# Attention feeding a channel mix: one ring of PSUM banks, dense dummy matmuls, a re-ordered plan and re-cut loads

## The chip, the cores and the metric

The kernel runs on one core of a Trainium2 chip. The metric is device time in microseconds (us), the median of several executions. One execution was also profiled; its trace gives every instruction's start and duration on the engines: TensorE (PE, matmuls; PEld for its weight loads), VectorE (DVE), ScalarE (ACT), GpSimd (POOL) and SyncE (SP, which here only issues transfers).

## What is computed

There are 8 batches of 576 tokens and 8 heads of 64 columns. `phi` gives 32 memory slots per head. The output of the attention, with heads side by side, goes through a token-shift channel mix with weights of 512 x 1024, 1024 x 512 and 512 x 512.

```python
def _attn_ref(q, k, v, phi):
    a = np.exp(phi - np.max(phi, axis=2, keepdims=True))
    a = a / (np.sum(a, axis=2, keepdims=True) + 1e-09)       # over the tokens
    k_m = np.einsum('bhsm,bhsd->bhmd', a, k)
    v_m = np.einsum('bhsm,bhsd->bhmd', a, v)
    scores = np.matmul(q, k_m.transpose(0, 1, 3, 2)) / np.sqrt(64)
    attn = softmax(scores)                                   # over the 32 slots
    return np.matmul(attn, v_m)

def _moe_ref(x, mu_k, mu_r, w_k, w_v, w_r):
    x_prev = x shifted by one token
    xk = mu_k * x + (1.0 - mu_k) * x_prev
    xr = mu_r * x + (1.0 - mu_r) * x_prev
    k = np.maximum(xk @ w_k, 0.0)
    v = k * k @ w_v
    r = 1.0 / (1.0 + np.exp(-(xr @ w_r)))
    return r * v
```

## The kernel before

**Two families of steps.** `attention(b)` (L212) makes the steps of one batch, `channel_mix(c)` (L512) those of one chunk of 512 tokens; there are nine chunks. The list `PLAN` (L18) is a hand-kept order of all steps: `0:hk0` is step `hk0` of batch 0, `c0:12` the thirteenth step of chunk 0. The program is recorded in just this order, so every engine executes its own instructions in the order of `PLAN`; semaphores make them wait for their operands and for free buffers.

**A batch's steps.** `exp` (L229) takes the exponential of phi on ACT, `exp0` and `exp1` each for 64 of the 128 partitions. `k`, `v`, `kv` (L232) sum keys and values over the tokens on PE, 72 small matmuls; `hk0`, `hk1`, `hv0`, `hv1` do so for half the heads. `z` (L248), or `z0` and `z1` (L256), is the sum of the exponentials, 9 matmuls each. `nk`, `nv`, `hn0`, `hn1` divide on DVE; `tk`, `ht0`, `ht1` (L295) transpose the memory keys. `q0` and `q1` (L318), or `hq0` and `hq1` (L333), transpose the queries on PE, 18 matmuls each, and copy them out of PSUM; `hq` puts one of its two copies on ACT, `q` puts all on DVE but for batch 0. `qx` (L313) does the same for batch 7 with two crossbar transfers that SP issues. `s0` and `s1` (L348) are the scores with their exponentials on ACT. `l0` to `l3` (L366) sum over the slots on PE and take Ln on ACT; `r0z`, `h0z` and the like (L378) take Exp of minus that, the reciprocal; `w`, `y` (L383) multiply on DVE. From batch 2 on, `x0` to `x3` (L390) are the attention's output, copied out by ACT, and `dd`, `k0d`, `k2d`, `r0d`, `r2d` (L404, L415) form the two token-shift mixes on DVE. For batches 0 and 1 `mk0` to `mk3` and `mr0` to `mr3` (L435) fold the mix into the value product on PE ("mixed value matmuls"), and half of their copies are on ACT, half on DVE.

**A chunk's steps.** Steps 0 to 7 are keys (L518): four matmuls, Relu on ACT into `rl`, the square on DVE into `sq`. Gates (L534): four matmuls, Exp on ACT, and after every second one Ln and Exp of 1024 columns on ACT. Values (L551): eight matmuls, a multiply on DVE into `o`, a store that SP issues. In chunks 0 and 8 steps 8 to 11 are the gates and 12 to 15 the values; in the others they alternate in pairs.

**Dummies.** `busy1` (L192) is one matmul of 128 x 512 zeros whose result nobody reads.

**Buffers.** [...] They are three pools, `at` of 3, `pk` of 2, `pv` of 3; keys and dummies use `pk`, gates and values `pv`, and the attention's tiles whatever the letters after a `+` in `PLAN` name (L215). Most attention tiles in SBUF have two buffers, `sq` one.

**Loads.** POOL issues them all, with a cast to bf16, but for batch 0's phi. Before any step: k and q of batch 0 by halves, v, `wk` in two pieces, `wr`, `wv`, then batch 1 (`ORDER`, L46). `b:load` (L291) loads batch b+2 into the buffers of b. At most eight POOL loads are under way: each waits for the one eight before it.

Of the kernel before, what the change touches and what calls it, by code (L numbers as in the profile page):

```python
# [18 lines left out]
    "0:exp0 0:busy1 0:busy1 0:busy1 0:busy1 0:busy1 0:busy1 0:exp1 0:z0 0:hk0+k 0:busy1 0:hn0 0:ht0+v 0:hq0+va",  # L19
    "0:z1+v 0:busy1 0:s0+kv 0:hk1+v 0:busy1 0:l0 0:busy1 0:h0z 0:busy1 0:l1 0:hn1 0:ht1+k 0:mu+k 0:hq1+vv 0:mub",  # L20
    "0:h1z 0:y1 0:s1+va 0:hv0+v 0:nr0 0:busy1 0:l2 0:h2z 0:nk0 0:y0 0:l3 0:y2 0:busy1 6:load 0:busy1 0:h3z 0:busy1",
    "0:hv1+v 0:nk1 0:y3 0:load 0:busy1 0:mk1+aa 0:nr1 0:mk0+ka 0:mk2+vk 0:mk3+va 0:mr0+av c0:0 c0:1 c0:2 c0:3 c0:4",
    "c0:5 c0:6 c0:7 0:mr2+aa 0:mr1+va c0:8 0:mr3+kk 1:exp c0:9 c0:10 c0:11 0:busy1 1:z+k 0:busy1 c0:12 1:k+aa 1:nk",
    "1:tk 1:q1+aa 1:q0+av c0:13 1:s1+kv 1:s0+kv 1:v+aa 1:nk1 1:nr0 1:nk0 1:nr1 1:l2+v 1:load 1:h2z 1:y2 1:l3 1:h3z",
    "1:y3 c0:14 7:load 1:l1+v 1:l0 1:h1z 1:y1 1:h0z 1:y0 c0:15 2:exp 1:mk1+av 1:mk2+vk 1:mk0+ak 2:z 1:mk3+av",
    "1:mr0+vv c1:0 c1:1 c1:2 1:mr3+aa 1:mr1+va 1:mr2+vv c1:3 2:q0+ak 2:q1+av 2:kv+vv 2:nk c1:4 c1:5 2:load 2:tk",
    "3:exp 2:nv c1:6 c1:7 2:s0+aa 2:s1+av c1:8 c1:9 2:l2+k c1:10 2:l3+v c1:11 2:r1z 2:w1 3:z+k 2:l0 2:l1+k 3:q1+va",
    "2:r0z c1:12 2:x3+vk 2:x2+aa 3:kv+vk 2:w0 2:x1+va 3:nv 3:nk 3:q0+kv 3:load 2:x0+av 3:tk c1:13 3:s0+ka 2:dd",
    "2:k0d 3:s1+ak 2:k2d 4:exp c1:14 c1:15 3:l0+v 2:r2d c2:0 c2:1 4:z 3:l1 c2:2 c2:3 2:r0d c2:4 3:r0z 3:l3 c2:5",
    "3:l2 c2:6 4:kv+va 4:nk 3:r1z 3:w1 4:nv 5:exp c2:7 c2:8 c2:9 3:w0 4:q1+av 4:q0+ak 4:load c2:10 3:x2+vk 3:x1+ka",  # L30
# [15 lines left out]
ORDER = ('wv', 'phi', 'k', 'q', 'v')  # L46

NJ = 9
# [4 lines left out]
def kernel(  # L56
# [94 lines left out]
    wk_v = moe_w_k.rearrange("(do di) f -> di do f", di=128)  # L151
    for i in range(2):
        fs = slice(i * Dff // 2, (i + 1) * Dff // 2)
        nc.gpsimd.dma_start(out=wk_sb[:, :, fs], in_=wk_v[:, :, fs])
    nc.gpsimd.dma_start(out=wr_sb, in_=moe_w_r.rearrange("(do di) d2 -> di do d2", di=128))
    wv_v = moe_w_v.rearrange("(fo fi) d -> fi fo d", fi=128)
    for what in ORDER:
        if what == "wv":
            nc.gpsimd.dma_start(out=wv_sb, in_=wv_v)
        elif what == "phi":  # L160
            load_phi(1, (nc.gpsimd, nc.gpsimd))
        elif what == "q":
            load_q(1)
        else:
            load_rows(kvs[1][:, "kv".index(what)], (k, v)["kv".index(what)][1])


# [24 lines left out]
    def keep_busy(n):  # L192

        ps = psum.tile([128, CT], F32, name="idle", tag="pk", bufs=2)
        for _ in range(n):
            nc.tensor.matmul(ps, lhsT=zeros[:, 0:128], rhs=zeros, start=True, stop=True,  # L196
                             skip_group_check=True)

    def load_mu_b():
        ps = psum.tile([128, 2, 2, D], F32, name="mub", tag="pk", bufs=2)  # L200
        for c in range(2):
            nc.tensor.matmul(ps[:, :, c], lhsT=sel[:, c].rearrange("k g m -> k (g m)"), rhs=mu_r[:, :, c],
                             start=True, stop=True, skip_group_check=True)
        nc.vector.tensor_copy(mu_m[:, :, 0], ps)
        nc.vector.tensor_scalar(mu_m[:, :, 1], ps, -1.0, 1.0, op0=AL.mult, op1=AL.add)

    def load_mu():
        ps_mu = psum.tile([128, 2 * ND], F32, name="psmu", tag="at", bufs=3)
        nc.tensor.transpose(ps_mu, mu2, ident_f)
        nc.vector.tensor_scalar_add(mu1, ps_mu, -1.0)  # L210

    def attention(b):  # L212
        st = {}

        def ps_tile(shape, dtype, name):  # L215

            tags = st["tags"]
            tag = {"a": "at", "k": "pk", "v": "pv"}[tags[st["n"] % len(tags)]]
            st["n"] += 1
            return psum.tile(shape, dtype, name=name, tag=tag, bufs={"at": 3, "pk": 2, "pv": 3}[tag])  # L220
# [27 lines left out]
        def esum():  # L248
            st["zps"] = ps_tile([128, 2], F32, "zps")
            for j in range(NJ):  # L250
                nc.tensor.matmul(st["zps"], lhsT=em[:, j].rearrange("p h m -> p (h m)"), rhs=ones,
                                 start=j == 0, stop=j == NJ - 1, skip_group_check=True)
            st["rz"] = work.tile([128, 2], F32, name="rz", tag="rz")
            nc.vector.reciprocal(st["rz"], st["zps"])

        def esum_half(c):  # L256

            def go():
# [5 lines left out]
                if "rz" not in st:  # L264
                    st["rz"] = work.tile([128, 2], F32, name="rz", tag="rz")
# [3 lines left out]
        def norm_k(cs=(0, 1)):  # L269

            def go():
                if "kbd" not in st:
                    st["kbd"] = work.tile([128, 2, 2, D], BF16, name="kbd", tag="kbd")
# [5 lines left out]
        def norm_v():  # L279
            vb = work.tile([128, 2, D], BF16, name="vb", tag="vb")  # L280
# [14 lines left out]
        def tr_k(cs=(0, 1)):  # L295

            def go():
# [5 lines left out]
                if "kmT" not in st:  # L303
                    st["kmT"] = work.tile([128, 2, 128], BF16, name="kmT", tag="kmT")
# [13 lines left out]
        def tr_q(i):  # L318
            def go():
# [8 lines left out]
                for hg in range(2):  # L328
                    (nc.scalar.copy if b == 0 and hg else nc.vector.tensor_copy)(
# [18 lines left out]
        def scores(c):  # L348

            def go():  # L350
                if "e" not in st:
                    st["e"] = work.tile([128, 2, S], BF16, name="e", tag="e")
# [30 lines left out]
        def weigh(c, sl=slice(0, S)):  # L383
            def go():
                if "at" not in st:
                    st["at"] = work.tile([128, 2, S], BF16, name="atn", tag="atn")
# [3 lines left out]
        def values(c, hf):  # L390

            def go():
                if "x" not in st:
                    st["x"] = work.tile([128, ND, S], BF16, name="x", tag="x")
# [90 lines left out]
        def step(name):  # L485
            name, _, tag = name.partition("+")
# [3 lines left out]
            def go():  # L490
                st["tags"], st["n"] = tag or "a", 0
                steps[name]()
            return go
# [18 lines left out]
    def channel_mix(c):  # L512
# [5 lines left out]
        def key(fi):  # L518
            def go():
                if "sq" not in st:  # L520
                    st["sq"] = work.tile([128, NF, CT], BF16, name="sq", tag="sq", bufs=1)
                pk = psum.tile([128, CT], F32, name="pk", tag="pk", bufs=2)
# [11 lines left out]
        def gate(ts):  # L534

            def go():
                pr = psum.tile([128, Dm], F32, name="pr", tag="pv", bufs=3)
# [13 lines left out]
        def value(ts):  # L551
            def go():
                o = work.tile([128, Dm], F32, name="o", tag="o", bufs=4)
                n = 2 if c == NCH - 1 and ts == 3 else 1
                for h in range(n):
                    cols = slice(h * Dm // n, (h + 1) * Dm // n)
                    pv = psum.tile([128, Dm], F32, name="pv", tag="pv", bufs=3)
# [7 lines left out]
        groups = [key(fi) for fi in range(NF)]  # L565
        order = "g0 g1 g2 g3 v0 v1 v2 v3" if c in (0, NCH - 1) else "g0 g1 v0 v1 g2 g3 v2 v3"
        return groups + [(gate if o[0] == "g" else value)(int(o[1])) for o in order.split()]


# [41 lines left out]
```

## Time and profile before

| | |
|---|---|
| median of 5 runs | 213.32 us (212.94 to 213.4) |
| the profiled execution | 213.26 us |
| its span, first to last instruction | 211.5 us |
| mean granted clock of PE | 0.968 |
| PE busy | 202.0 us, 96% |
| ACT busy | 161.4 us, 76% |
| DVE busy | 136.0 us, 64% |
| POOL busy | 46.2 us, 22% |
| moved by DMA | 31.90 MB, mean 151 GB/s |

The span is 1.76 us shorter than the time of the same execution: what lies ahead of the first instruction and after the last belongs to the time only. "Busy" counts a matmul from its start to its modelled end, and matmuls overlap, so 96% doesn't say that PE works at its peak. The granted clock is the share of full speed that PE was allowed. DMA is busy throughout the first half of the span and mostly at four tenths or less after it.

### The profile page before, as it was taken

How to read it: one execution, taken by the hardware profiler on the slowest of the kernel's cores; microseconds unless marked ns; L12 is line 12 of the kernel's file. 1: busy time of each engine (PE TensorE's matmuls, PEld its weight loads, DVE VectorE, ACT ScalarE, POOL GpSimd, SP SyncE). 2: the span in 40 equal slices, each digit the busy share in tenths (PEclk: the TensorE clock that was granted, in tenths of full speed). 3: DMA queues.
4: the chain of work that ended last, by engine and by line, in shares of the span. 5: the costliest groups of instructions: out<-in, count | busy, mean ns of one | idle time of the engine just before them, and what ended most of it. 6: DMA issues, size and time to landing. Idle time of an engine off the chain costs nothing.

```text
span 211.5 us, 5608 instructions
## 1 busy us (share of the span) xinstructions
PE 202.0 (96%) x2268; PEld 101.3 (48%) x2268; DVE 136.0 (64%) x338; ACT 161.4 (76%) x304; POOL 46.2 (22%) x79
## 2 busy tenths in 40 slices
PE   5699999999999999999999999999999999999992
PEld 1465434555454454544546855444444444444451
DVE  1326651796729988599869776975797497524231
ACT  2555779596698989887979799699979966766760
POOL 7732144532645352444200000000000000000000
PEclk9755999999999999999999999999999999999999
DMA  6999999999999999999991744030421034044024
GB/s 134 209 206 206 229 208 216 240 238 303 209 244 235 246 242 228 231 240 245 241 213 55 142 66 102 13 86 0 102 63 41 10 89 102 0 99 99 0 69 133
DMA packets 25826, 31.90 MB, mean 151 GB/s; under 512 B 4800, under 2 KB 20424, under 8 KB 25800
## 3 DMA queue, kind: packets, MB, share of 16 engines
q0 software_dynamic: 16912, 20.91, 53.9%
q1 hardware_dynamic: 8360, 10.07, 18.8%
q10 hardware_dynamic: 528, 0.56, 1.0%
q8 instruction: 18, 0.29, 0.5%
q14 instruction: 8, 0.07, 0.1%
HBM read 38.28 MB, written 9.44 MB: 226 GB/s over the span
## 4 chain that ended last, share of the span: by engine, by line
PE 88%; ACT 5%; DMA 3%; issue 1%; DVE 1%; POOL 0%; ACTq 0%; POOLq 0%
PE pk L526 29%; PE pv L559 28%; PE pr L540 14%; PE kvps L242 3%; DMA q<-in_q_dram 3%; PE idle L196 2%; PE mxps L288 2%; PE zps L373 2%; PE qtps L325 2%; PE nops L288 1%; PE scps L359 1%; PE qtps L341 1%; ACT rl L530 1%; ACT sg L545 1%; ACT x L399 1%
## 5 line engine op out<-in xcount | busy, mean ns | idle before, releaser
L559 PE MATMUL pv<-wv,sq 128*128 128x512 bf16 (+1 forms) x296 | 66.7, 374 | 0.0
L526 PE MATMUL pk<-xkT,wk 128*128 128x512 bf16 (+1 forms) x320 | 66.4, 358 | 0.0
L530 ACT ACTIVATE rl<-pk 128x512 bf16<-128x512 f32 x72 | 42.5, 600 | 20.8 <-PE pk L526 17.8
L526 PEld LDWEIGHTS <-wk 128*128 128x128 bf16 x320 | 30.6, 98 | 28.8 <-issue 0.9
L531 DVE TENSOR_TENSOR sq<-rl 128x512 bf16<-128x512 bf16 x72 | 29.9, 424 | 20.5 <-ACT rl L530 19.7
L559 PEld LDWEIGHTS <-sq 128*128 128x128 bf16 x296 | 28.1, 98 | 31.3 <-issue 0.6
L561 DVE TENSOR_TENSOR o<-sg,pv 128x512 f32<-128x512 f32 (+1 forms) x37 | 24.3, 670 | 27.8 <-ACT sg L548 15.5
L540 PE MATMUL pr<-wr,xrT 128*128 128x512 bf16 x144 | 34.9, 380 | 0.2 <-DVE xrT L447 0.2
L545 ACT ACTIVATE sg<-pr 128x512 f32<-128x512 f32 x36 | 21.3, 616 | 4.9 <-PE pr L540 4.7
L540 PEld LDWEIGHTS <-xrT 128*128 128x128 bf16 x144 | 13.2, 98 | 16.2 <-issue 0.6
L548 ACT ACTIVATE sg<-sg 128x1024 f32<-128x1024 f32 x18 | 19.0, 1057 | 0.6
L547 ACT ACTIVATE sg<-sg 128x1024 f32<-128x1024 f32 x18 | 19.0, 1057 | 0.6
L399 ACT CAST x<-nops 128x256 bf16<-128x256 f32 (+1 forms) x48 | 15.5, 418 | 2.4 <-PE nops L288 2.2
L421 DVE TENSOR_SCALAR mu_d<-diff,mu 128x576 bf16<-128x576 bf16 x48 | 15.6, 369 | 0.2
L118 POOL DMA_DIRECT2D kv<-in_k_dram x16 | 10.1, 629 | 21.3 <-DMA kv<-in_k_dram 3.8
L387 DVE TENSOR_TENSOR atn<-e,lz 128x576 bf16<-128x576 bf16 (+2 forms) x20 | 12.6, 635 | 2.0 <-ACT lz L380 1.7
L363 ACT ACTIVATE e<-scps 128x320 bf16<-128x320 f32 (+1 forms) x32 | 10.9, 429 | 3.5 <-PE scps L359 3.4
L118 POOL DMA_DIRECT2D q<-in_q_dram x16 | 9.8, 613 | 16.8 <-PE qtps L325 4.3
L375 ACT ACTIVATE lz<-zps 128x320 f32<-128x320 f32 (+1 forms) x32 | 12.2, 409 | 1.3 <-PE zps L373 1.1
L118 POOL DMA_DIRECT2D kv<-in_v_dram x16 | 9.8, 613 | 15.4 <-DMA wv<-in_moe_w_v_dram 4.5
L230 ACT ACTIVATE em<-ph 128x1152 bf16<-128x1152 f32 (+1 forms) x9 | 10.5, 1169 | 2.6 <-DMA ph<-in_phi_dram 2.6
L380 ACT ACTIVATE lz<-lz 128x576 f32<-128x576 f32 (+2 forms) x20 | 11.7, 592 | 0.3
(65 smaller groups left out, 172.7 us busy)
## 6 DMA issues: line engine op xcount, KB each, us to landing
out_dram<-o SPq DMA_DIRECT2D x69, 128.0 KB, 3.6
kv<-in_k_dram POOLq DMA_DIRECT2D x16, 288.0 KB, 9.8
q<-in_q_dram POOLq DMA_DIRECT2D x16, 288.0 KB, 10.3
kv<-in_v_dram POOLq DMA_DIRECT2D x16, 288.0 KB, 9.6
ph<-in_phi_dram POOLq DMA_DIRECT2D x7, 288.0 KB, 11.1
ph<-in_phi_dram POOLq DMA_DIRECT2D x14, 144.0 KB, 10.9
wk<-in_moe_w_k_dram POOLq DMA_DIRECT2D x2, 512.0 KB, 12.9
wv<-in_moe_w_v_dram POOLq DMA_DIRECT2D x1, 1024.0 KB, 18.9
```

The costliest lines, as they stand in the source:

```text
L118: nc.gpsimd.dma_start(out=dst[ROWS[hg]].rearrange("p h j d -> p h (j d)"), in_=rows(src, hg))
L399: nc.scalar.copy(st["x"][:, 2 * c + jj, sl], pss[jj])
L421: nc.vector.tensor_scalar_mul(t[:, i], st["d"][:, pr + i, :], mu1[:, o:o + 1])
L526: nc.tensor.matmul(pk[:, lo:hi], lhsT=wk_sb[:, di, fi * 128:(fi + 1) * 128], rhs=xk_T[:, di, c0:c0 + hi - lo], start=(di == 0), stop=(di = ...
L530: nc.scalar.activation(rl, pk, AF.Relu)
L531: nc.vector.tensor_mul(st["sq"][:, fi, :], rl, rl)
L540: nc.tensor.matmul(pr, lhsT=xr_T[:, di, c0:c0 + 128], rhs=wr_sb[:, di, :], start=(di == 0), stop=(di == ND - 1))
L545: nc.scalar.activation(sg[:, ts % 2], pr, AF.Exp, scale=-1.0)
L547: nc.scalar.activation(sg, sg, AF.Ln, bias=1.0)
L548: nc.scalar.activation(sg, sg, AF.Exp, scale=-1.0)
L559: nc.tensor.matmul(pv[:, cols], lhsT=st["sq"][:, fi, ts * 128:(ts + 1) * 128], rhs=wv_sb[:, fi, cols], start=(fi == 0), stop=(fi == NF - 1))
L561: nc.vector.tensor_mul(o[:, cols], st[ts // 2][:, ts % 2, cols], pv[:, cols])
```

## The change

- `PLAN` is written anew. Batch 0 begins with 13 dummies instead of 6; six more stand later in the head, and six in the stretch where chunk 0 ends and batch 1 begins (two before). Batch 1 takes its exponentials, sums, keys, values and queries by halves (`exp0`, `z0`, `hk0`, `hq0`). Batch 6's queries go by crossbar (`6:qx`), as batch 7's do.
- All PSUM tiles come from one pool of eight; the letters in `PLAN` are gone.
- Eight SBUF tiles get three buffers instead of two, `sq` two instead of one.
- The loads before the steps follow a list, `PRE`: `wk` in three pieces, `wr`, then batch 1's q, phi and k, and `wv` in two halves of 256 columns around batch 1's v.
- Chunk 0's values are made and stored by halves of 256 columns, steps 12 to 19.
- In all chunks steps 8 to 11 are now the gates and 12 on the values.

```diff
 PLAN = [
-    "0:exp0 0:busy1 0:busy1 0:busy1 0:busy1 0:busy1 0:busy1 0:exp1 0:z0 0:hk0+k 0:busy1 0:hn0 0:ht0+v 0:hq0+va",
-    "0:z1+v 0:busy1 0:s0+kv 0:hk1+v 0:busy1 0:l0 0:busy1 0:h0z 0:busy1 0:l1 0:hn1 0:ht1+k 0:mu+k 0:hq1+vv 0:mub",
-    "0:h1z 0:y1 0:s1+va 0:hv0+v 0:nr0 0:busy1 0:l2 0:h2z 0:nk0 0:y0 0:l3 0:y2 0:busy1 6:load 0:busy1 0:h3z 0:busy1",
-    "0:hv1+v 0:nk1 0:y3 0:load 0:busy1 0:mk1+aa 0:nr1 0:mk0+ka 0:mk2+vk 0:mk3+va 0:mr0+av c0:0 c0:1 c0:2 c0:3 c0:4",
-    "c0:5 c0:6 c0:7 0:mr2+aa 0:mr1+va c0:8 0:mr3+kk 1:exp c0:9 c0:10 c0:11 0:busy1 1:z+k 0:busy1 c0:12 1:k+aa 1:nk",
-    "1:tk 1:q1+aa 1:q0+av c0:13 1:s1+kv 1:s0+kv 1:v+aa 1:nk1 1:nr0 1:nk0 1:nr1 1:l2+v 1:load 1:h2z 1:y2 1:l3 1:h3z",
-    "1:y3 c0:14 7:load 1:l1+v 1:l0 1:h1z 1:y1 1:h0z 1:y0 c0:15 2:exp 1:mk1+av 1:mk2+vk 1:mk0+ak 2:z 1:mk3+av",
...
+    "0:busy1 0:busy1 0:exp0 0:busy1 0:busy1 0:busy1 0:busy1 0:busy1 0:busy1 0:busy1 0:busy1 0:busy1 0:busy1 0:busy1",
+    "0:hk0 0:z0 0:hn0 0:exp1 0:hq0 0:ht0 0:busy1 0:z1 0:s0 0:hk1 0:busy1 0:l0 0:hn1 0:busy1 0:h0z 0:l1 0:ht1 0:mu",
+    "0:hq1 0:mub 0:s1 7:load 0:h1z 0:hv0 0:nk0 0:nr0 0:y1 0:busy1 0:y0 0:l2 0:h2z 0:busy1 0:busy1 0:l3 0:h3z 0:y2",
+    "0:hv1 0:nk1 0:y3 0:mk1 0:mk0 0:mr0 0:mk3 0:mk2 c0:0 0:nr1 c0:1 c0:3 c0:2 0:mr1 0:mr2 c0:6 c0:4 c0:5 c0:7 c0:8",
+    "0:mr3 1:exp0 1:exp1 c0:10 c0:11 1:hq1 1:z0 0:load 1:hq0 c0:9 0:busy1 1:z1 1:hk0 1:hn0 0:busy1 1:hk1 0:busy1",
+    "0:busy1 0:busy1 1:hn1 1:ht1 0:busy1 1:ht0 1:s1 1:s0 c0:17 6:load c0:13 1:hv0 1:nr0 1:l0 1:h0z 1:l1 1:h1z 1:y0",
+    "1:l3 1:y1 1:l2 1:hv1 1:nk0 1:load 1:h2z 1:y2 1:h3z 1:y3 1:nk1 c0:15 1:nr1 c0:19 1:mk0 1:mr0 c0:12 c0:16 c0:18",
+    "c0:14 1:mk1 1:mk3 1:mk2 1:mr2 c1:6 c1:3 2:exp c1:5 c1:0 c1:7 c1:4 c1:2 c1:1 c1:8 2:z 1:mr3 1:mr1 2:kv 2:nk",
...
+    "c3:12 c3:13 c4:1 c4:6 c4:4 5:tk c4:3 c4:2 6:z 6:kv 6:nk 5:s0 5:s1 6:nv c4:8 c4:7 5:l3 6:qx 5:l2 5:l0 4:r2d",
+    "5:l1 5:r1z 5:w1 5:r0z 5:w0 7:qx 4:r0d c4:5 c4:0 c3:14 5:x2 5:x1 c3:15 5:x0 5:x3 5:dd 5:k0d 5:k2d c4:10 7:exp",
...
 ]
-ORDER = ('wv', 'phi', 'k', 'q', 'v')
+PRE = "k0:0 q0:0 k1:0 q1:0 id: v0:0 v1:0 wk:0-2 wk:2-4 wk:4-8 wr:0-4 q1:1 phi:1 q0:1 k0:1 k1:1 wv:2-4 v0:1 v1:1 wv:0-2"
...
+    def preload(word):
+
+        what, _, part = word.partition(":")
+        if what in weights:
+            dst, src = weights[what]
+            f0, f1 = (int(x) * 128 for x in part.split("-"))
+            nc.gpsimd.dma_start(out=dst[:, :, f0:f1], in_=src[:, :, f0:f1])
+        elif what == "id":
+            make_identity(nc, identity)
         else:
-            load_rows(kvs[1][:, "kv".index(what)], (k, v)["kv".index(what)][1])
+            n = int(part)
+            if what == "phi":
+                load_phi(n, (nc.gpsimd, nc.gpsimd))
+            elif what[0] == "q":
+                load_q(n, (int(what[1]),))
+            else:
+                load_rows(kvs[n][:, "kv".index(what[0])], (k, v)["kv".index(what[0])][n], (int(what[1]),))
+
+    for word in PRE.split():
+        preload(word)
...
         def ps_tile(shape, dtype, name):
-
-            tags = st["tags"]
-            tag = {"a": "at", "k": "pk", "v": "pv"}[tags[st["n"] % len(tags)]]
-            st["n"] += 1
-            return psum.tile(shape, dtype, name=name, tag=tag, bufs={"at": 3, "pk": 2, "pv": 3}[tag])
+            return psum.tile(shape, dtype, name=name, tag="ps", bufs=8)
...
-                    (nc.scalar.copy if b == 0 and hg else nc.vector.tensor_copy)(
+                    (nc.scalar.copy if b < 2 and hg else nc.vector.tensor_copy)(
...
-                    st["sq"] = work.tile([128, NF, CT], BF16, name="sq", tag="sq", bufs=1)
-                pk = psum.tile([128, CT], F32, name="pk", tag="pk", bufs=2)
+                    st["sq"] = work.tile([128, NF, CT], BF16, name="sq", tag="sq", bufs=2)
+                pk = psum.tile([128, CT], F32, name="pk", tag="ps", bufs=8)
...
-        def value(ts):
-            def go():
-                o = work.tile([128, Dm], F32, name="o", tag="o", bufs=4)
-                n = 2 if c == NCH - 1 and ts == 3 else 1
-                for h in range(n):
+        def value(ts, hs=(0,), n=1):
+
+            def go():
+                if ("o", ts) not in st:
+                    st["o", ts] = work.tile([128, Dm], F32, name="o", tag="o", bufs=4)
+                o = st["o", ts]
+                for h in hs:
                     cols = slice(h * Dm // n, (h + 1) * Dm // n)
-                    pv = psum.tile([128, Dm], F32, name="pv", tag="pv", bufs=3)
+                    pv = psum.tile([128, Dm], F32, name="pv", tag="ps", bufs=8)
...
-        groups = [key(fi) for fi in range(NF)]
-        order = "g0 g1 g2 g3 v0 v1 v2 v3" if c in (0, NCH - 1) else "g0 g1 v0 v1 g2 g3 v2 v3"
-        return groups + [(gate if o[0] == "g" else value)(int(o[1])) for o in order.split()]
+        if c == 0:
+            values = [value(ts, (h,), 2) for ts in range(4) for h in range(2)]
+        elif c == NCH - 1:
+            values = [value(ts) for ts in range(3)] + [value(3, (0, 1), 2)]
+        else:
+            values = [value(ts) for ts in range(4)]
+        return [key(fi) for fi in range(NF)] + [gate(ts) for ts in range(4)] + values
```

## Prediction

> **What bounds the kernel now.** I read the page first, then the chain of waits in order of time, then windows, then the timeline of the head. On the page, busy time, the slices of the granted clock and the shares of the chain:
>
> ```profile
> PE 202.0 (96%) x2268; PEld 101.3 (48%) x2268; DVE 136.0 (64%) x338; ACT 161.4 (76%) x304; POOL 46.2 (22%) x79
> PEclk9755999999999999999999999999999999999999
> PE 88%; ACT 5%; DMA 3%; issue 1%; DVE 1%; POOL 0%; ACTq 0%; POOLq 0%
> ```
>
> TensorE (PE) is both busy and the chain, and its clock is low in slices 2 to 4 only. The chain gives the borders of four stages (start, length, what):
>
> ```profile
> 1.97 6.52 DMA q<-in_q_dram
> ...
> 21.89 7.10 PE pk L526 x32
> ...
> 45.70 0.70 PE mxps L288 x28
> ...
> 200.35 7.00 PE pv L559 x40
> 207.35 0.02 issue
> 207.37 0.42 DVE o L561
> ```
>
> Stage A, 0 to 21.89, ends with the first key matmul of chunk 0. B, 23.81 us, ends at batch 1's first mixed value matmul. C, 161.65 us, is steady: 32 full key matmuls in 6.9 us are 216 ns each, and no gap above 0.4 us stands in it. D, 4.14 us, is the last multiply and its store. B holds 21.8 us of PE work at those spacings (keys 6.9, gates 3.5, values 6.9, batch 0's last mixed halves 1.0, batch 1's sums, transposes and scores 3.1, dummies 0.4), so PE loses 2.0 us there, most of it at 29.5 to 30.5 and 36.8 to 38.2. An edit can pay in A, in B, or by taking matmuls out of C.
>
> Why A is slow, by windows of 3.41 us (window, length, PE busy and instructions, granted clock, DMA share, GB/s):
>
> ```profile
> 0.80:4.22 3.42, 2.74 (x6) 1.00 0.58 142
> 4.22:7.63 3.41, 1.08 (x46) 1.00 1.22 211
> 7.63:11.05 3.42, 2.81 (x71) 0.50 1.21 206
> 14.46:17.87 3.41, 3.41 (x56) 0.50 1.24 205
> 17.87:21.29 3.42, 3.42 (x82) 0.50 1.24 205
> 21.29:24.70 3.41, 3.41 (x31) 1.00 1.25 209
> 205.60:209.02 3.42, 1.73 (x16) 1.00 0.72 187
> 209.02:211.49 2.47, 0.00 (x0) 1.00 0.22 66
> ```
>
> The clock is halved exactly after the window that is 32% busy and comes back at 21.29. The window at the end that is 51% busy isn't followed by a halving. The head's timeline shows what left that second window empty:
>
> ```profile
> 1.19 2.74 PE L196 MATMUL idle<-zeros 128*128 128x512 bf16 x6 [1.19 <-DVE zeros L138]
> 6.49 0.38 PE L261 MATMUL zps<-ones,em 64*128 64x1 bf16 x9 [2.55 <-ACT em L230]
> 8.53 0.98 PE L341 MATMUL qtps<-identity,q 64*128 64x64 bf16 x15 [0.51 <-DMA q<-in_q_dram]
> ```
>
> Six dummies end at 3.9 and PE then waits for the exponential of phi until 6.5.
>
> [...]
>
> **The change, stage by stage.**
>
> A, if the clock holds. Thirteen dummies from 1.19 us: seven at 0.43 us to 4.2, six at 0.216 to 5.5. Then `hk0` and `z0` at 6.48 (they still wait for phi's exponential, 5.27 + 1.16). Window 4.22 to 7.63 is then 1.3 + 0.6 = 1.9 us busy, 56%; the next I count at 53%. Both lie above the 51% that kept the clock. Queries land at 8.48 as now, since the first loads keep their order. From there, with PE at half its time and the rest at trace durations: 18 transposes 0.4, ScalarE (ACT) copy 0.64 and latency, so `s0` at 9.85 (now 10.14); exponentials to 10.95; `l0`, Ln and reciprocal to 12.0; Ln of `l1`, ACT copy of the second queries to 13.0; `s1` 13.05; exponentials to 14.15; four ACT steps for rows 2 and 3 to 16.25; VectorE weighing (0.42) to 16.8; two mixed halves of 0.28. First key at **17.4**: -4.5. The gain is more than faster matmuls, since four of ten dummies inside this chain are gone, and the others are half as long.
>
> A, if it does not: the same chain at half clock, fewer dummies: first key at about 21.1, -0.8.
>
> B is where the price is. Work that leaves B: two of chunk 0's four value groups (four halves, 3.5 us). Work that enters: four more dummies (0.9) and nine more sums (9 x 0.025 = 0.2). PE work 19.3 us against 21.8. But the order puts these on ACT between gate `c0:8` and batch 1's score exponentials: gate 0.6, cast 0.4, exp of phi in two halves (1.16 each; L230 shows that 64 partitions cost as much as 128), gates 2 x 0.6, Ln and Exp of 1.06 each, two query copies of 0.64 that stood on VectorE, gate 0.6, Ln and Exp again. That is 10.6 us; successive ACT entries overlap a little, so 10.1. `c0:8` ends 8.9 us after the first key (eight keys 6.9, gate 0.86, two mixed 0.7, one wait 0.4), so exponentials start at 19.2 and the third, which `l0` needs, ends at 20.1. Then sums 0.7, `hv1` 0.3, two half-values 1.74: mixed at **22.9**. Against 23.81: -0.9, though PE now waits 3.6 us there. Who waits: `ht1`, `s1`, `l0`, and all PE work behind them. It is the ring of eight that ties `ht0` to a bank that the ACT copy must empty.
>
> Loads in B: wr landed at 22.6 (7.04 + 15.6) and wv, 1 MB, 5.1 us later. Now 1.77 MB (q, phi, k) follow wr: 8 us at about 225 GB/s, k complete at 30.5; `hk1` needs it near 31.6 and has a further 1 us before ACT binds. wv's first half lands about 33.0 (wanted 35.0), its second about 38 (wanted 41). No stall taken; bounded at 0 (nothing in B waits for a load now, so none can be gained) [...]. On POOL wv now stands behind batch 1's loads; the loads of later batches keep their order, since `0:load` only moves against other engines.
>
> C: the 3.5 us from B return. Batch 6's queries by crossbar take out 36 transposes, 0.63 us by the chain, and four VectorE copies of 0.45 off the path. Two crossbar issues (about 1.7 us each on SP) join the two for batch 7; stores wait behind them, with four output buffers as cover, and both are issued some 20 us before use. If batch 7's queries landed after their turn, stores and then VectorE's multiplies would queue: bounded at 0 to +1. The mixing chain of VectorE leaves about 0.2 us of new hole ahead of chunks 2 and 5. C = 161.65 + 3.5 - 0.63 + 0.2 = **164.7**. At nothing: one pool, deeper buffers, two squares buffers (PE never waits in C; bounds -0.4, the holes there, to +1, since a tile may now wait for the eighth tile before it); VectorE's eight half multiplies for four (+0.6 us, hidden under PE); twice the stores of chunk 0; two more POOL issues of 0.6 us, under the DMA stream. If PE stops being the cover, ACT with 161 us is the next.
>
> D is unchanged, 4.14.
>
> Sum: 17.4 + 22.9 + 164.7 + 4.1 = 209.1 against a span of 211.5. The profiled execution took 213.26, 1.76 above its span, and the median is 213.32, 0.06 more. So **210.9**, or -1.1%.
>
> **The rivals.**
>
> 1. Clock lost halfway (window 7.63 to 11.05 too thin, its matmuls small): A near 20.1, so +2.7 on the forecast: 213.6. For: windows full of small matmuls at half clock did not bring the clock back. Against: 51% held it.
>
> 2. Slower: the dummies don't hold the clock at 7.63. A is then 21.1, and B and C cost 187.6 where they cost 185.5 now: 21.1 + 22.9 + 164.7 + 4.1 = 212.8, time 214.6, with B up to 1 us worse. It decides once A gains less than 2.1 us. For: 56% was not seen followed by a kept clock while the matmuls were 64 rows tall. This is also the case that the change doesn't do what it says.
>
> 3. Clock held, but weights in pieces or a slow ACT chain stretch B by 2 to 3 us: 213 to 214. For: loads saturate DMA in B (share 1.18). Against: the margins above, 1 to 3 us.
>
> **How the numbers follow.** Forecast 0.52, rival 1 0.15, rival 2 0.25, rival 3 0.08. No change is within 0.2%, 0.4 us, about what a measurement of this kernel can tell. The forecast's own range is 209.2 to 212.6: A +-0.6, B -1 to +1, C -0.4 to +1. Faster: 0.49 + 0.06 + 0.02 + 0.01 = 0.58. Same: 0.02 + 0.03 = 0.05. Slower: 0.37. The range runs from 209.0 to 215.0 and leaves out a tenth on each side.
>
> **What would show it.** Right: PEclk at full in slices 2 to 4, first key near 17.4, ACT without gaps for 10 us before batch 1's scores, PE holes of 3 to 4 us there, 36 fewer transposes. Wrong: half clock after 7.6; batch 1 waiting for k or wv; holes after 46 us.

## The result and the profile after

The changed kernel took 213.50 us in the median of 27 runs (210.13 to 214.48), the kernel before 213.34 us in 48 (212.59 to 215.49): over all runs there is no difference. The ratio on record, 0.9939 with an interval of [0.9917, 0.9961], counts only fast runs, those within 1.5% of the kernel's fastest, and so leaves out 19 of the changed kernel's 28; it is no evidence of a gain in the usual run. The runs of the changed kernel differ by the clock that TensorE was granted. With every run's recorded mean clock beside its time (the 27 and the profiled one):

| recorded clock | runs | time, us | span, us |
|---|---|---|---|
| 1.0 | 2 | 210.13, 210.20 | 208.4, 208.3 |
| 0.980, 0.981 | 3 | 212.09 to 212.24 | 210.3 to 210.5 |
| 0.972 to 0.976 | 18 | 212.88 to 213.85 | 211.1 to 212.1 |
| 0.968 | 5, the profiled one among them | 214.22 to 214.56 | 212.4 to 212.8 |

A window of 3.41 us at half clock lowers the mean over the span by 0.008. So 0.968 is four such windows, as in the profile below (13.65 us); 0.972 to 0.976 is about three and 0.980 about two, an estimate, since no other run of this kernel was profiled. By the times of the table each costs about 1 us. The mean alone proves little, because it counts the time ahead of the first entry of the record as full speed (see e3): runs of the kernel before have means of 0.962 to 1.0 at the same times.

So the profile below (time 214.56, span 212.8) is of a run that lost the clock as early as the kernel before did. What the two runs without a loss look like inside is taken from an experiment, e1, whose span is the same within 0.3 us. Busy times, slices of the granted clock and shares of the chain, after:

```profile
PE 204.2 (96%) x2280; PEld 106.4 (50%) x2280; DVE 134.6 (63%) x338; ACT 162.3 (76%) x307; POOL 47.9 (23%) x81
PEclk9755999999999999999999999999999999999999
PE 87%; ACT 6%; DMA 3%; issue 1%; DVE 1%; POOL 0%; ACTq 0%; POOLq 0%
```

TensorE is still the busy engine and the chain, and slices 2 to 4 are at a low clock as before. The borders of the stages in the chain of waits (start, length, what), after:

```profile
1.97 6.76 DMA q<-in_q_dram
...
21.44 3.80 PE pk L519 x16
...
44.86 0.67 PE mxps L285 x24
...
201.95 6.94 PE pv L554 x40
...
208.91 0.42 DVE o L556
```

Stage A is 0.45 us shorter than before (21.44 against 21.89), B 0.39 shorter (23.42 against 23.81), C 2.38 longer (164.03 against 161.65: it got 3.5 us of chunk 0's values and lost batch 6's transposes), D 0.24 shorter: +1.3 us in the span. The windows of the head (window, length, busy time and instructions of PE, PEld, VectorE, ScalarE and POOL, granted clock, DMA share, GB/s) show where the clock went, after:

```profile
1.41:4.82 3.41, 3.41 (x9) 1.21 (x8) 0.28 (x4) 1.28 (x1) 3.33 (x7) 1.00 0.81 177
4.82:8.23 3.41, 1.88 (x50) 0.94 (x48) 1.42 (x12) 1.98 (x2) 3.00 (x5) 1.00 1.21 213
8.23:11.65 3.42, 2.88 (x73) 2.17 (x73) 0.85 (x3) 1.28 (x3) 1.68 (x3) 0.50 1.21 206
```

In the first of them the dummies come 0.43 us apart, against 0.22 from 4.92 us on: half clock, though it is printed as full (see e3). The thirteen dummies end at 5.95 us, TensorE waits 0.8 us for the keys and 1.27 for the queries, and behind a window that was 55% busy the clock is at half for 13.65 us, to 21.9 us. Stage B, in the chain of waits, is a row of ScalarE work, as forecast:

```profile
33.25 1.08 ACT sg L538 x2
...
34.35 1.06 ACT sg L540
...
35.44 1.06 ACT sg L541
36.50 1.07 ACT qT L341 x2
37.56 0.51 ACT sg L538
...
38.09 1.07 ACT sg L540
...
39.19 1.06 ACT sg L541
40.24 0.93 ACT e L360 x3
```

### The profile page after: what moved, and what is told of

Same layout as the page of the kernel before. It is cut to its first block, busy times and chain, and to the rows that moved or that the text cites. A ratio compares the mean times of both kernels' runs of the same rounds, so it can differ in the third digit from the quotient of the medians.

```text
span 212.8 us, 5653 instructions
## 1 busy us (share of the span) xinstructions
PE 204.2 (96%) x2280; PEld 106.4 (50%) x2280; DVE 134.6 (63%) x338; ACT 162.3 (76%) x307; POOL 47.9 (23%) x81
## 4 chain that ended last, share of the span: by engine, by line
PE 87%; ACT 6%; DMA 3%; issue 1%; DVE 1%; POOL 0%; ACTq 0%; POOLq 0%
PE pk L519 28%; PE pv L554 28%; PE pr L533 15%; DMA q<-in_q_dram 3%; PE kvps L239 3%; PE mxps L285 2%; PE zps L370 2%; PE nops L285 2%; ACT sg L540 2%; ACT sg L538 1%; PE qtps L338 1%; PE idle L197 1%; PE qtps L322 1%; PE scps L356 1%; ACT sg L541 1%
## 5 line engine op out<-in xcount | busy, mean ns | idle before, releaser
L523 ACT ACTIVATE rl<-pk 128x512 bf16<-128x512 f32 x72 | 40.0, 599 | 8.3 <-PE pk L519 8.0
L554 PEld LDWEIGHTS <-sq 128*128 128x128 bf16 x328 | 31.3, 98 | 29.1 <-issue 0.5
L519 PEld LDWEIGHTS <-wk 128*128 128x128 bf16 x320 | 30.8, 98 | 29.9 <-issue 0.8
L556 DVE TENSOR_TENSOR o<-sg,pv 128x512 f32<-128x512 f32 (+1 forms) x41 | 24.9, 619 | 19.0 <-ACT sg L541 9.9
L114 POOL DMA_DIRECT2D kv<-in_k_dram x16 | 10.1, 631 | 21.1 <-PE kvps L239 8.8
L227 ACT ACTIVATE em<-ph 128x1152 bf16<-128x1152 f32 (+1 forms) x10 | 11.6, 1163 | 2.8 <-DMA ph<-in_phi_dram 2.8
L372 ACT ACTIVATE lz<-zps 128x320 f32<-128x320 f32 (+1 forms) x32 | 11.5, 414 | 1.2 <-PE zps L370 1.0
```

The lines of the kernel that those rows point to most:

```text
L114: nc.gpsimd.dma_start(out=dst[ROWS[hg]].rearrange("p h j d -> p h (j d)"), in_=rows(src, hg))
L519: nc.tensor.matmul(pk[:, lo:hi], lhsT=wk_sb[:, di, fi * 128:(fi + 1) * 128], rhs=xk_T[:, di, c0:c0 + hi - lo], start=(di == 0), stop=(di = ...
L523: nc.scalar.activation(rl, pk, AF.Relu)
L554: nc.tensor.matmul(pv[:, cols], lhsT=st["sq"][:, fi, ts * 128:(ts + 1) * 128], rhs=wv_sb[:, fi, cols], start=(fi == 0), stop=(fi == NF - 1))
L556: nc.vector.tensor_mul(o[:, cols], st[ts // 2][:, ts % 2, cols], pv[:, cols])
```

## The experiments

Theory at the start: the time of the changed kernel is decided by whether dummies and small matmuls fill the 3.4 us windows between 4.8 and 11 us, and everything else in the change costs 1.3 us net. Rival: the clock is chance, and the order, the pool and the loads carry what gain there is. The second half of the theory fell with e2. All stages at a glance (first key, batch 1's first mixed value, end of the last values, span; profiled run, us) with the median of each. "First key" is where the key matmuls run on without a stop; in e1, e3, e4, e6, e8, e9 and e11 up to three single ones come up to 1.1 us earlier, and in e12 a row of four counts:

| kernel | first key | mixed | last value | span | median |
|---|---|---|---|---|---|
| before | 21.89 | 45.70 | 207.35 | 211.5 | 213.34 |
| after | 21.44 | 44.86 | 208.89 | 212.8 | 213.50 |
| e1, head filled | 18.56 | 40.53 | 204.72 | 208.6 | 210.62 |
| e2, before with head filled | 18.47 | 45.88 | 207.55 | 211.6 | 213.29 |
| e3, six dummies | 21.79 | 44.38 | 208.40 | 212.3 | 214.18 |
| e4, e1 with less on ScalarE | 19.23 | 40.68 | 205.23 | 209.1 | 210.36 |
| e5, e2 with wv last | 18.70 | 49.88 | 211.42 | 215.4 | 217.24 |
| e6, e1 with the loads of before | 19.04 | 48.84 | 213.48 | 217.3 | 220.13 |
| e7, e4 with dummies out | 20.15 | 42.58 | 206.92 | 210.8 | 211.40 |
| e8, e1 without crossbar for batch 6 | 18.83 | 40.81 | 206.54 | 210.5 | 212.61 |
| e9, e4 with crossbar for batch 5 | 20.16 | 41.39 | 209.90 | 213.7 | 218.18 |
| e10, e1 with two rings of four | 19.84 | 46.02 | 230.14 | 234.0 | 236.79 |
| e11, e1 with whole values | 18.72 | 53.30 | 213.58 | 217.5 | 217.53 |
| e12, e4 with VectorE's row cut | 17.47 | 39.87 | 204.71 | 208.6 | 210.37 |

### e1: fill the waits of the head

```diff
-0:busy1 0:busy1 0:exp0 0:busy1 (11 times)
-0:hk0 0:z0 0:hn0 0:exp1 0:hq0 0:ht0 0:busy1 0:z1
+0:busy1 0:busy1 0:exp0 0:busy1 (11 times) 0:busy3
+0:hk0 0:z0 0:busy5 0:hn0 0:exp1 0:hq0 0:ht0 0:busy2 0:z1
```

> Edit: only dummies are added in the head of the changed kernel: three more before hk0 (16 in place of 13), five between z0 and hn0, where TensorE waits 1.27 us for the queries, and one more ahead of z1. Theory (the clock is decided by how full TensorE's 3.4 us windows are between 4.8 and 11 us): no halved window in any run, first key near 17.4 us (21.44 with the clock lost), span 208.3, time 210.1 +-0.3 in all runs. Rival (the clock is a matter of chance, or windows of small matmuls count as idle whatever is put between): runs spread from 210 to 214.5 as those of the changed kernel do, median 213.4.

Measured: 210.62 us (210.35 to 211.25, 4 runs; before 213.26), ratio 0.9878 [0.9854, 0.9901]. All four lie below 211.3 us, as only 2 of 28 did without the fill; three are above the expected 209.8 to 210.4. Windows of e1's head, columns as above:

```profile
4.89:8.30 3.41, 3.20 (x56) 1.64 (x56) 1.37 (x11) 1.93 (x2) 2.94 (x5) 1.00 1.21 217
8.30:11.71 3.41, 3.41 (x82) 2.03 (x80) 1.17 (x4) 2.05 (x5) 1.62 (x3) 1.00 1.21 206
```

94% busy where the changed kernel had 55%, and full clock behind it. Compared matmul by matmul, the changed kernel's profiled run falls behind e1 from 9.3 us on (0.6 us there, 2.6 at the second scores, 3.9 at the first key) and stays 3.7 to 4.3 behind to the end: the whole difference of 4.2 us in the span arises in the head. Filling paid, and the clock is not chance: e4, e8 and e12, which keep this head, have 14 more runs, all with a recorded mean of 0.996 or more and within each kernel less than 1 us apart. The first key matmul came at 17.43, as expected, but the group stopped twice for casts and ran on at 18.56 (start, length, from TensorE's timeline; in brackets the idle time and what ended it):

```profile
17.43 0.39 PE L519 MATMUL pk<-xkT,wk 128*128 128x512 bf16 x1
18.01 0.38 PE L519 MATMUL pk<-xkT,wk 128*128 128x512 bf16 x1 [0.19 <-ACT xkT L444]
18.56 2.97 PE L519 MATMUL pk<-xkT,wk 128*128 128x512 bf16 x13 [0.17 <-DVE xkT L444]
```

The chain shows VectorE at the end of A in e1:

```profile
13.20 0.42 DVE mu_m L205
...
14.07 0.61 DVE vm L427 x2
14.68 0.82 DVE atn L384 x2
...
16.65 0.73 DVE xkT L444 x2
17.38 0.40 DVE xrT L444
17.78 0.74 DVE xkT L444 x2
```

### e2: the filled head on the kernel before

```diff
-0:busy1 0:busy1 0:exp1 0:z0 0:hk0+k 0:busy1 0:hn0
+0:busy1 0:busy1 0:busy10 0:exp1 0:z0 0:hk0+k 0:busy5 0:hn0
```

> Edit: the kernel before with a filled head and nothing else of the change: 16 dummies ahead of the first sums in place of 6, five more between hk0 and hn0. Theory (the dense head is all that the change gains by, and its other parts cost 1.3 us net: B only 0.4 shorter, C 2.4 longer): clock held, first key near 17.9 us, the rest 189.6 us as before, span 207.5, time 209.3, so about 1 us faster than e1_fill. Rival (the other parts pay once the clock is held): 210.4 or more, slower than e1_fill. If the clock is lost: 213.3.

Measured: 213.29 us (212.59 to 214.72, 14 runs; before 213.26), ratio 1.0015 [0.9993, 1.0037]. The time is the rival's, 210.4 or more. In the profiled run the clock was held and the first key came 3.4 us earlier, but B grew by 3.6, from 23.81 to 27.41. In the chain of e2 (lines of the kernel before):

```profile
14.61 16.21 DMA ph<-in_phi_dram
...
30.93 1.16 ACT em L230
...
45.88 0.70 PE mxps L288 x28
```

Batch 1's phi is queued behind wk, wr and the whole of wv, and lands at 30.8 us whatever TensorE does. In the kernel before it landed at 30.5 and ScalarE began on it at 31.7, so of the 3.4 us only 1.2 were to be had there. Six of the 14 runs (214.26 to 214.72, recorded clock 0.991 or 0.992) seem to have lost one window; the other eight have a median of 213.0. This refutes "all else costs 1.3 us": with the clock held, all else gains 2.7 us (the medians of e2 and e1), or 2.4 with those eight. Dense dummies alone are worth nothing here, 0.3 us at most.

### e3: six dummies in the changed kernel

```diff
-0:busy1 0:busy1 0:exp0 0:busy1 (11 times)
+0:busy1 0:busy1 0:exp0 0:busy1 (4 times)
```

> Edit: the changed kernel with 6 dummies ahead of hk0 in place of 13, as before has them. Theory: four halved windows in every run as in the kernel before, first key 21.4 to 21.9, time 214.3 to 214.8, no run under 214: the thirteen dummies are what moves most runs of the changed kernel to 212 to 213.8, and all else costs 1.3 us. Rival (the thirteen dummies do nothing in most runs): the same spread as the changed kernel, median 213.5.

Measured: 214.18 us (213.87 to 214.47, 8 runs; before 213.26), ratio 1.0044 [1.0029, 1.0059]. That is just under the expected 214.3 to 214.8, with one run at 213.87 where none under 214 was expected. The thirteen dummies thus are worth 0.7 us in the median, and 4 where they hold the clock. From e3's page, and from its chain of waits:

```profile
PEclk9999999999999999999999999999999999999999
...
8.91 1.14 PE qtps L338 x18
```

The clock line is full all through, yet eighteen transposes take 1.14 us, as in the changed kernel at half clock, against 0.64 in e1. The record of granted clocks in this trace begins only at 20.2 us, and what lies ahead of it is printed as full. In the changed kernel's trace it begins at 4.82 us, where the dummies go from 0.43 us apart to 0.22, and in that of the kernel before at 4.22, behind the first six dummies. So in this run the clock was not lost, as I expected, but never came up before 20.2 us; three other runs, with a recorded mean of 0.967 or 0.968, took 214.08 to 214.43 us, this one 214.06. Where the record doesn't reach, the length of the matmuls is the evidence.

### e4: less ScalarE work in stage B

```diff
-1:exp0 1:exp1
+1:exp
-(nc.scalar.copy if i else nc.vector.tensor_copy)(        # tr_q_half
+(nc.scalar.copy if b == 0 and i else nc.vector.tensor_copy)(
-(nc.scalar.copy if b < 2 and hg else nc.vector.tensor_copy)(   # tr_q
+(nc.scalar.copy if b == 0 and hg else nc.vector.tensor_copy)(
```

> Edit: e1_fill with batch 1's exponential of phi in one instruction in place of two halves (ScalarE -1.16 us) and batch 1's query copies all on VectorE (ScalarE -1.07 us). Theory (stage B is bound by the row of ScalarE work between gate c0:8 and batch 1's score exponentials): B shrinks from 23.4 to about 21.4 us, C unchanged at 164.0, time 2.0 us under e1_fill, 208.1 if the clock is held. Rival (B is bound by the loads of batch 1 or by TensorE's own work): B 22.8 to 23.4, time within 0.6 us of e1_fill.

Measured: 210.36 us (209.99 to 210.88, 4 runs; before 213.26), ratio 0.9863 [0.984, 0.9886]; its interval covers e1's ratio, as the rival said. B went from 21.97 to 21.45 us, not by the 2.0 expected. Scores ran at 34.4 and exponentials at 34.8, when ScalarE came free; then TensorE's own order (two value halves, `hv0`, the sums) stood ahead of the rest. ScalarE's row was the longest, but only by half a microsecond. C was 0.4 longer; see e12.

### e5 and e6: the loads

```diff
 e5 (on e2)
-ORDER = ('wv', 'phi', 'k', 'q', 'v')
+ORDER = ('phi', 'k', 'q', 'wv', 'v')
 e6 (on e1)
-PRE = "... wk:0-2 wk:2-4 wk:4-8 wr:0-4 q1:1 phi:1 q0:1 k0:1 k1:1 wv:2-4 v0:1 v1:1 wv:0-2"
+PRE = "... wk:0-4 wk:4-8 wr:0-4 wv:0-4 phi:1 k0:1 k1:1 q0:1 q1:1 v0:1 v1:1"
```

> Edit: e2_before_fill (the kernel before with a filled head) with batch 1's phi, k and q loaded ahead of wv instead of behind it; nothing else. Background: in e2 the head gained 3.4 us and stage B lost 3.6, because batch 1's phi landed at 30.8 us whatever the clock did. Theory (load order and the order of chunk 0's values only pay together): phi now lands near 26 us, but wv, 1 MB whole, near 36, and chunk 0's first value group stands in TensorE's order ahead of batch 1's sums; batch 1's first mixed value at 46 to 47 us, time 213.3 to 214.5, no gain. Rival (phi's landing alone held stage B): mixed near 42, time 209.5.

> Edit: e1_fill with the loads of before put back: wk in two pieces, wr, wv whole, then batch 1's phi, k, q, v. Theory (what the change gains in stage B is that batch 1's phi lands at 26.9 and not at 30.8 us): ScalarE's exponential of phi starts at 30.9 in place of 27.3, everything behind it is 3.6 us later, batch 1's first mixed value at 44.1 us (40.5 in e1_fill), time 214.2. Rival (the new instruction order and the single pool carry the gain, the loads are hidden): time within 0.6 us of e1_fill, 210.6.

Measured: e5 217.24 us (217.12 to 217.77, 4 runs; before 213.42), ratio 1.0181 [1.0161, 1.02]; e6 220.13 us (219.17 to 221.0, 4 runs), ratio 1.031 [1.0276, 1.0344]. From the chain of e5:

```profile
23.21 12.87 DMA wv<-in_moe_w_v_dram
36.08 0.05 issue
36.13 3.32 PE pv L559 x8
```

wv landed at 36.1, as expected, and TensorE stood for it through the whole window from 32.2 to 35.6; the clock was halved behind that, so eight value matmuls took 3.32 us in place of 1.73, and mixed came at 49.9, 3 us past the expectation. In e6 the wait is for another load than I expected, in its chain:

```profile
22.80 13.27 DMA q<-in_q_dram
36.07 0.05 issue
36.12 0.96 PE qtps L338 x16
```

phi landed at 30.9 as expected, but the changed order takes batch 1's queries first, and in these loads they come behind phi and the keys, at 34.6 and 36.1; again the clock was lost in the wait (33.7 to 40.5). The new order of instructions with the old loads thus costs 9.5 us (e6 against e1), and batch 1 ahead of a whole wv doesn't pay in the old order (e5, which is only a part of the new loads). Order and loads fit each other. How much of the 8.3 us by which mixed is later in e6 a single load carries was not separated.

### e8: batch 6's queries by TensorE again

```diff
-6:qx
+6:q1 6:q0
```

> Edit: e1_fill with batch 6's queries transposed by TensorE again (two steps of 18 matmuls at the place of the crossbar issue). Theory (C is TensorE's own work without holes): 36 transposes add 0.63 us to C, 164.2 to 164.8, time 211.2. Rival (the crossbar transfers cost the stores and the chain what they save): C unchanged, time 210.6.

Measured: 212.61 us (212.26 to 212.99, 6 runs; before 213.42), ratio 0.9957 [0.994, 0.9973]. C is 1.54 us longer than in e1 (165.73 against 164.19), where 0.63 was expected. The same matmuls are 0.45 us late just ahead of the transposes, 1.19 just behind, and 1.82 from 120 us on: 0.74 arise at the transposes and 0.63 at a stop between two half-values (119.7), with an idle wait of 0.33 us. VectorE has the four query copies more; among the waits from 112 to 122 us of e8 is:

```profile
PE nops L285 <- DVE atn L384: 0.3, 1, 0.3
```

So the crossbar step takes out transposes and a VectorE delay that reached TensorE.

### e11: chunk 0's values whole

```diff
-values = [value(ts, (h,), 2) for ts in range(4) for h in range(2)]
+values = [(value(ts) if h else (lambda: None)) for ts in range(4) for h in range(2)]
```

> Edit: e1_fill with chunk 0's values in four whole groups of 512 columns, each at the place of its first half; wv still loads in two column halves, the second landing at 39.3 us. Theory (the halves are what lets the values run before wv is complete): TensorE stands at the first value group (34.6 us in e1_fill) until 39.3, 4.7 us, and then works 3.7 us more ahead of batch 1's first mixed value: 48.5 to 49.5 us in place of 40.5; C gives the 3.7 back: time 214.5 to 216, more if the clock is lost in the wait. Rival (the halves only split work): mixed at 44.2, C 160.5, time 210.6 to 211.

Measured: 217.53 us (216.82 to 219.23, 4 runs; before 213.57), ratio 1.0169 [1.0116, 1.0222]. From its chain:

```profile
26.96 13.64 DMA wv<-in_moe_w_v_dram
40.60 0.14 issue
40.74 6.52 PE pv L554 x16
```

TensorE stood 5.8 us for the second half of wv, lost the clock (36.4 to 46.7 us), and came to batch 1's mixed values at 53.3, later than expected by the lost clock; C gave 3.9 us back. Value halves and column halves of wv are one edit: without the first the second brings a wait. Both left whole wasn't tried.

### e10: two rings of four banks

```diff
-return psum.tile(shape, dtype, name=name, tag="ps", bufs=8)
+return psum.tile(shape, dtype, name=name, tag="at", bufs=4)   # the other tiles: tag="ps", bufs=4
```

> Edit: e1_fill with the one pool of eight PSUM banks split in two rings of four: attention's tiles in one, chunk's and dummies' in the other. Theory (which bank a tile gets is worth nothing in C, where TensorE never waited for one, and little in the head): C 164.2 +-0.4, batch 1's first mixed value 40.5 to 41.5 us, time 210.6 to 211.6. Rival (the instruction order needs the eight): in the head and in stage B attention has up to six tiles under way, so holes of 2 to 4 us there, and some in C: time 213 or more.

Measured: 236.79 us (235.79 to 239.28, 4 runs; before 213.57), ratio 1.1099 [1.1031, 1.1168]. This was my largest miss. The windows of stage C (columns as above), e10 first, then e1:

```profile
46.02:230.14 184.12, 172.38 (x1651) 86.52 (x1650) 115.20 (x269) 133.72 (x250) 25.87 (x42) 1.00 0.61 123
```

```profile
40.53:204.72 164.19, 163.03 (x1632) 83.67 (x1650) 115.22 (x274) 131.88 (x252) 28.27 (x46) 1.00 0.71 145
```

The work of VectorE and ScalarE is the same within 2 us, but C is 20 us longer. TensorE, which had 0.5 us at most ahead of any group in e1's C, now sits idle 11.6 us in all ahead of nine of them. Its busy time grows by some 9 us too, though the mean length of a matmul stays: the small matmuls that overlapped in e1 now overlap less (the 96 of `nops` take 7.6 us where they took 4.4, at 0.30 us each in both). Three of the groups of e10's C (group, count, busy time and mean, idle before it and what ended it):

```profile
L519 PE MATMUL pk<-xkT,wk 128*128 128x512 bf16 (+1 forms) x288 | 59.3, 355 | 3.5 <-ACT rl L523 2.0 <-DVE o L556 1.5
...
L356 PE MATMUL scps<-qT,kmT 64*32 64x320 bf16 (+1 forms) x96 | 4.5, 290 | 2.3 <-ACT e L360 2.1 <-DVE rz L251 0.2
...
L322 PE MATMUL qtps<-identity,q 64*128 64x64 bf16 x144 | 4.2, 190 | 2.0 <-DVE qT L326 1.7
```

These releasers are the instructions that empty a bank of the same small ring. One such row in the chain of e10, where a key group waits for a bank that a value holds until its gates are through ScalarE:

```profile
122.44 0.49 ACT sg L538
122.96 1.07 ACT sg L540
124.05 1.06 ACT sg L541
125.14 0.70 DVE o L556
125.88 1.03 PE pk L519 x8
```

The order of the change doesn't stand this split; one ring of eight serves it. What the hand-given tags of the kernel before would cost or gain under the new order wasn't tried.

### e7, e9 and e12: attempts at a better version

```diff
 e7 (on e4): the six 0:busy1 between 1:hq0 and 1:ht0 left out;  0:hk1 0:busy1 -> 0:hk1 0:mub;  0:hq1 0:mub 0:s1 -> 0:hq1 0:s1
 e9 (on e4): 0:hk1 0:busy1 -> 0:hk1 0:mub;  0:hq1 0:mub 0:s1 -> 0:hq1 0:busy3 0:s1;  5:q0 5:nv 5:q1 -> 5:qx 5:nv
 e12 (on e4): 0:mk1 0:mk0 0:mr0 0:mk3 0:mk2 c0:0 -> 0:mk1 0:mk0 0:mk3 0:mk2 c0:0 0:mr0;  nc.scalar.copy(mu_m[:, :, 0], ps)
```

> Edit: e4_fill_act without the six dummies that stand between batch 1's first sums in stage B (1.3 us of TensorE), and with the two matmuls of mub moved from ahead of s1 to just behind hk1, so that VectorE makes its two copies (0.42 and 0.34 us) at 11 to 12 us where it is idle. Theory (with ScalarE's row cut, B is TensorE's own work, dummies included, and A ends in VectorE's row from 13.2 to 18.5 us): first key 0.7 earlier, near 17.9 us; B 20.6 to 21.0 (ScalarE takes over as the bound after half of the gain); time 209.0 to 209.4. Rival (both rows only fill waits that something else ends): time that of e4_fill_act, 210.2 to 210.5.

> Edit: e4_fill_act with mub's two matmuls moved to just behind hk1 and three dummies left in their old place ahead of s1 (e7 thinned these windows and lost the clock at 14.1 us), and batch 5's queries by the crossbar too, as batches 6 and 7. Theory: VectorE's two copies of mu_m (0.76 us) leave the row that ends A, first key near 18.0 us (19.2 in e4's profile, of which 0.7 was a late start); the crossbar takes 0.63 us of transposes out of C and, as e8 showed, up to 0.9 us of waits: C 163.0 to 163.9; time 208.6 to 209.4. Rival (mub's copies and the transposes of batch 5 only fill waits): 210.2 to 210.5. If the clock is lost again: first key after 19.5 us.

> Edit: e4_fill_act with the first copy of mu_m on ScalarE in place of VectorE, and chunk 0's mixed half mr0, which only the gates need, moved from ahead of mk3 to just behind the first key group c0:0. Theory (with the clock held, stage A ends in VectorE's row: copy 0.42, copy 0.34, vm, atn, casts from 13.2 to 18.5 us in e1_fill, of which the key groups don't need the copy's place nor mr0's cast of 0.40): the key groups run without a stop from 17.8 us in place of 18.56, B unchanged, time 0.7 under e4_fill_act: 209.6 to 209.8. Rival (something else ends A, such as the loads of batch 0 or ScalarE's casts): 210.2 to 210.5.

Measured: e7 211.40 us (211.02 to 212.58, 6 runs; before 213.42), ratio 0.9899 [0.988, 0.9917]; e9 218.18 us (215.43 to 220.48, 6 runs; before 213.57), ratio 1.017 [1.0113, 1.0228]; e12 210.37 us (210.35 to 210.46, 4 runs; before 213.14), ratio 0.9865 [0.9848, 0.9882].

e7 missed: the clock was lost at 14.1 us, after a window that was 76% busy, and B did not shrink (22.4 us), which fits dummies in B that only fill waits. e9 missed twice. VectorE's early copies of `mu_m` stood ahead of the keys' scaling, and the first key came at 20.2. And the crossbar transfers of batch 5 ran beside the load stream: its queries had landed by 88.9 us, but the 2304 packets of 256 bytes took from 95.6 to 115.3 us. In e1 the same number for batch 6, begun behind the last load (112.7), took from 113.3 to 118.1. The second issue stood on SP for 10 us (start, length, from SP's timeline), and TensorE waited 3.2 us from 112.7 to 116.0 for the transposed tile and then lost the clock for a window:

```profile
93.82 10.10 SPq L312 DMA_TRANSPOSE qT<-q  x1
```

Batch 6's crossbar in the change meets no such wait: it is issued at 116.2 us, behind the last load. e12's time is the rival's, 210.2 to 210.5, yet it did what was meant in A and B: the first four key matmuls came at 17.47 and mixed at 39.87, 0.7 ahead of e1. Then its chain meets the load stream, which e1's does not:

```profile
51.35 9.62 DMA q<-in_q_dram
60.97 0.05 issue
61.01 0.70 PE qtps L322 x35
```

It ends at 204.71, e1 at 204.72. With the clock held and B tight, batch 3's queries are what stands in the way first: 0.5 of e12's 0.7 us are gone behind them, at 61.6 us. e4's 0.5 us went elsewhere in C, at 97.25, where a gate waited 0.47 us for VectorE's mix (`xrT`, L419) and e1's did not. Of all kernels e4 and e12 are the fastest, 1.4% under the kernel before, and not separable from e1.

## Why the prediction was right and wrong

**Right for a held clock, wrong that it would hold.** 210.9 was for a held clock; two runs of 28 had it, at 210.13 and 210.20. The median of 213.5 lies inside the stated 209.0 to 215.0 only because the range had room for the rivals. The step that failed is "Both lie above the 51% that kept the clock". The fill was right, 56% forecast and 55% measured, but 55% did not keep the clock in the profiled run. The 51% was one window at the end of the kernel before, of 16 large value matmuls (1.73 us busy) and with no matmul behind it; it was carried over to a window of 50, most of them small (1.88 us; see the last section). I gave the lost clock 0.25, and its sum (21.1 + 22.9 + 164.7 + 4.1 = 212.8, time 214.6) met the profiled run's 21.44 + 23.42 + 164.03 + 3.91 = 212.8 and 214.56. That it met to 0.1 is luck: A and B were 0.3 and 0.5 too low, C and D 0.7 and 0.2 too high. Most runs lie between the two, at rival 1's 213.6, with a part of the loss; none of these was profiled, so that the clock was lost halfway in them is argued from the recorded mean clock, not seen.

**A with the clock held** was sized at 17.4, and e1's first key matmul starts at 17.43, with nine dummies more in its head. What no term had is the 1.1 us until the keys run on, at 18.56. I followed ScalarE and TensorE, and gave VectorE a single weighing: `mu_m`, `vm`, `atn` and the casts are a row from 13.2 to 18.5 us. e12, which takes two of its pieces out of the way, has four key matmuls in a row from 17.47. Also, `hk0` waits for its keys and not for phi's exponential: it started at 6.76, where 6.48 was predicted.

**B** was 22.9, measured 23.42. The ScalarE row was right to 0.4 us (exponentials at 18.8 us behind the first key, 19.2 predicted, though the terms, 8.9 + 10.1, give 19.0); sums and `hv1`, with a wait of 0.45 us between them, took 0.8 us more than I had. With the clock held B is 21.97 from 18.56, or 23.10 from the first key matmul, and A and B together 40.53 against 40.3 predicted.

**Loads.** Landings were right to 1.5 us: k 31.1 (30.5 predicted), wv 33.7 and 39.5 (33.0 and 38). No stall, as forecast. Wrong was the reason "nothing in B waits for a load now, so none can be gained": phi's slack in the kernel before was 1.2 us, and a head 3.4 us faster runs into it. In the kernel before, a faster head thus gained nothing (e2), and the new order with the old loads lost (e6). The two pieces of wv, 2048 packets of 512 bytes, landed 0.7 and 1.5 us behind the forecast, and no wait for them stands in the chain.

**C** was 164.7, measured 164.03, and 164.19 in e1. Of the terms, the crossbar was sized at 0.63 and is 1.5 (e8). "One pool at nothing" was right for the sum only: with two rings of four the new order is 26 us slower (e10). Deeper buffers were not tried apart.

**D** was 4.14, measured 3.91.

**Where the expected gain went**: into a clock that was lost all the same in 26 of 28 runs. Nine more dummies in the head make it 1.2%.

## What to carry to other kernels

When a faster stage is forecast, list what lands by itself in the next one, with its slack: the gain is cut to the smallest slack (1.2 us here), however certain it is. Order, loads and buffers of one plan belong together: undoing the loads (e6), the value halves (e11) or the one ring (e10) cost 7 to 26 us, where the whole plan with a filled head gains 2.7. A wait of TensorE was paid twice where its clock fell behind it (in e5 the next eight value matmuls took 3.32 us in place of 1.73), and nine dummies in the waits of the head took the median from 213.50 to 210.62 us (e1): fill the waits in the head, and look at the spread of single runs before believing a median.

## What was unexpected of the hardware

- The windows of the clock don't start with the kernel: taken back by steps of 3.41 us, their borders lay at 0.81 us in the profile before, 1.41 after, 1.48 in e1 and 0.5 in e7. That the same program can have its thin stretch in one window or across two, and that the changed kernel's runs spread by this, is an estimate: no two profiles of it were compared.
- The busy share of a window didn't decide. Half clock followed windows that were 0% busy in e5, 32% before, 50% in e11, 55% after and 76% in e7; it did not follow the one of 51% near the end of the kernel before, and in e2 the clock stayed at full from 18.47 to 45.88 us, though TensorE was idle for 4.36 us of them. What decides was not shown.
- A load that came late cost more than its wait, even in the middle of the kernel: the clock was at half for 3.4 us in e5, 6.8 in e6 and 10.2 in e11 (recorded means 0.992, 0.984 and 0.976), a part of it still in the wait. In e5 the eight value matmuls behind the wait took 1.6 us more (3.32 against 1.73).
